# A windowed attention and MLP mixer kernel on one Trainium2 core: batch 3's first channel product by seven products of quarters, and new orders for the work and the loads

## The chip, the core and the metric

The kernel runs on one core of one Trainium2 chip. Its time is the device time of one execution in microseconds (us). The kernel before took 197.43 us, the median of three runs (196.32 to 197.87). The core has a matrix engine, TensorE (PE, with its weight loads shown apart as PEld), and VectorE (DVE), ScalarE (ACT) and GpSimd (POOL), which work on elements; SyncE (SP) only issues DMAs here. Matrix products land in PSUM, which is divided into banks; all other tiles lie in SBUF. Each engine takes its own queue of instructions in order and waits where an instruction's inputs, or the tile that it writes, are not free.

## What is computed

Attention with a sliding window of 128 and 4 sink positions (B=4, H=8, S=768, D=64), whose result x (4 x 768 x 512) goes through an MLP mixer:

```python
scores = (1/sqrt(D)) * q @ k.T
keep = (pos < n_sink) | ((rel >= 0) & (rel < window))       # rel = query - key
a = softmax(where(keep, scores, -1e9));  x = a @ v          # heads side by side: 4 x 768 x 512
xt = x.transpose(0, 2, 1)
h = relu(xt @ w_tok1) @ w_tok2                              # w_tok1 768x256, w_tok2 256x768
u = x + h.transpose(0, 2, 1)
out = u + relu(u @ w_ch1) @ w_ch2                           # w_ch1 512x1536, w_ch2 1536x512
```

The inputs and the output are float32 in DRAM; the products are taken in bf16 with float32 sums. The four batches are computed independently of each other.

## The kernel before

**Attention.** The work is done by pairs of heads: p = 0 to 15, four pairs to a batch. GpSimd's queue loads q, k and v of a pair with a cast to bf16 (`load_cast` L136, `load_v` L144) and the weights (`load_w` L169); pairs 0 to 3 come in by SP in float32 and are cast on an engine (L160). SP's queue also transposes q and k of pairs 8 to 15 by DMA (`turned_by_dma` L429, the DMA at L438); TensorE transposes the others. For a pair there are three bursts of scores (`scores`; a burst of 4 x 128 keys and queries of two heads goes into one "sc" tile of two banks), an exponential on ACT (L596), a mask multiplication on DVE (L604), the scores of the sink keys, the products with v (`pv` L664, `values`), and the division by the row sums on DVE. `sink_rows` copies the sink rows of v of a pair to where the products read them (L158 on ACT, L160 on DVE); it needs that pair's v to have landed.

**Mixer.** `mix_h` and `mix_u` make the token mixing, DVE adds x (L813), and u is turned into uT, by TensorE or, for batches 2 and 3, by a DMA of SP's queue (`transfer_u` L867). The first channel product makes v1T = relu(w_ch1' uT), 12 row tiles of 128 times 768 columns, in 24 units of four matmuls of 128 x 384 (`v1`, about L990), each evicted with the rectification by ACT or DVE (`relu`, L164, L166). The second channel product is direct in batch 0 (`out_part`, added to u at L1014, stored at L1020). In batches 1, 2 and 3 (`QUARTERED`) it is made by quarters: the operands are cut in two by two blocks, and seven products of sums of blocks replace eight products of blocks. The sums of v1 (L1206, DVE) and of w_ch2 (`sums_of_w` L1224, once) are made ahead. The products 1 to 7, each for three row tiles a, b, c, go to partial sums in PSUM that several products write into one after the other: 1, 6, 7 and 4 accumulate in one half of a bank, 5 and 3 in the other half of the same bank, 2 in a bank of its own. Between them the state of such an open sum is read out by DVE and added to the output tiles (L1078); the outputs are stored from SP's queue (L1107). `PRODUCTS` (L69) is their order.

**What sets the order.** The whole program is written out by a planner (class `Plan`). Each piece of work is an `Op` with an estimated cost on each engine that may do it and a list of what it needs. The order on TensorE is fixed by hand in two lists: `FIRST_BATCH`, and `MERGED` (L48), in which c0, c1, ... are the units of `mix_channels` and t0, t1, ... those of `attention_and_tokens`. So c0 to c47 are batch 0's channel products, c48 to c92 batch 1's, c93 to c137 batch 2's, c138 to c182 batch 3's. `LOADS` (L64) fixes the order on GpSimd's load queue; in it v9 is the values of pair 9, T and A are w_tok1 and w_tok2, C0 to C3 and D0 to D3 the quarters of w_ch1 and w_ch2. Everything else is put on an engine when it is ready by the estimates, and then stays in that place of the engine's queue. PSUM holds two "sc" tiles of two banks and four "mx" banks; the planner gives a unit the bank that comes free first.

In MERGED the units that the prediction names are: t27, the second burst of pair 8; t28, the first of pair 9; t32, the first of pair 10, which also takes the products of the sink rows of pair 9; t64, the first burst of pair 15, in the changed order the last with scores; c104, a v1 unit of batch 2 that in the changed order comes soon after t64; h0, batch 0's first token mixing, the first use of w_tok1.

The end of the kernel is batch 3's second product. Its last four products are 7c, 4c and 3c after 6c; of the last row tile's outputs each 128 x 256 quarter is added and stored apart, four stores of 128 KB.

Of the kernel before, what the change touches and what calls it, by code (L numbers as in the profile page):

```python
# [16 lines left out]
def kernel(  # L17
# [47 lines left out]
        "v1 v2 T0 v3 A0 k4 q4 q5 C0 v4 k5 C2 v5 q6 C1 k6 C3 k7 q7 D0 q8 v6 k8 D2 D1 D3 v7 k9 q9 q10 v8 k10 "  # L65
        "k11 q11 v9 v10 k12 k13 q12 q13 v11 v12 k14 q14 v13 k15 q15 v14 v15"
# [5 lines left out]
    SUMMED = 3  # L72
    NQ = 6
# [30 lines left out]
    def rows_of(pidx, n):  # L104
# [10 lines left out]
        "p (g f s) -> p g f s", g=4, f=HF,  # L115
    )
# [98 lines left out]
    kTb = [singles.tile([P, S], BF16, name=f"kT{n}") for n in range(NKB)]  # L215
    qTb = [singles.tile([P, S], BF16, name=f"qT{n}") for n in range(NKB)]
    pTb = [singles.tile([P, 2, NT, 2, P], BF16, name=f"pT{n}") for n in range(NPT)]
# [65 lines left out]
    class Plan:  # L283
# [142 lines left out]

    QH = NT // 2
# [434 lines left out]
    def transfer_u(b, g):  # L862

        for s0, n in [(0, 4), (4, 2)] if g else [(0, NT)]:
# [9 lines left out]
            for half in range(s0 // QH, (s0 + n - 1) // QH + 1):  # L874
                done.setdefault(("uT", b, half), []).append(op)
            plan.pending.append(op)
# [102 lines left out]
    def mix_channels(b):  # L979
# [60 lines left out]

        def quartered(b):
# [4 lines left out]
            units, made = [], {}  # L1046
# [10 lines left out]
            def w_summed(n):  # L1057
# [7 lines left out]
            v1_deps = {  # L1065
                "1": (0, 0), "2": (0, 1), "4": (1, 1),
            }
            sum_of = {"3": 3, "5": 0, "6": 1, "7": 2}
            w_sum_of = {"4": 3, "5": 0, "6": 1, "7": 2}
            w_of = {"1": 0, "2": 1, "3": 1}  # L1070
            steps = {}

            def add(name, i, st, g, src, first):
                def run(e):
                    n = (b * NT + st) % NO
                    o_sb = o_buf[n][:, ts(g, QC)]
                    ps = tiles["ps_q", b, i][:, src] if src < 2 else tiles["ps_z", b, i]
                    in_order(nc.vector.tensor_tensor(  # L1078
                        out=o_sb, in0=ps, in1=u_rows(b, st)[:, g] if first else o_sb, op=ALU.add,
                    ))  # L1080

                op = Op({"DVE": 425.0}, run)
# [4 lines left out]
                steps[name, i] = op  # L1087
                return op

            for i in range(QH):  # L1090
                lo, hi = i, i + QH
                add("r1", i, lo, 0, 0, True)
                add("c1", i, lo, 0, 2, False)
                add("r2", i, lo, 1, 0, True)
                add("c2", i, lo, 1, 1, False)
                add("r4", i, hi, 1, 0, True)
                add("c4", i, hi, 1, 1, False)
                add("c3", i, hi, 0, 0, True)
                for later, sooner in (("c1", "r1"), ("c2", "r2"), ("c4", "r4")):
                    steps[later, i].deps.append(steps[sooner, i])  # L1100
                for st, parts in ((lo, ("c1", "c2")), (hi, ("c3", "c4"))):
                    last_one = b == B - 1 and i == QH - 1

                    def store(e, st=st, g=None):
                        o_sb = o_buf[(b * NT + st) % NO]
                        cols = slice(0, DM) if g is None else ts(g, QC)
                        in_order(nc.sync.dma_start(out=out[b, ds(st * P, P), cols], in_=o_sb[:, cols]))  # L1107

                    if last_one:
                        for part in parts:  # L1110
                            g = 0 if part in ("c1", "c3") else 1
                            op = Op({"SP": 100.0}, lambda e, st=st, g=g: store(e, st, g), [steps[part, i]])
# [16 lines left out]
            def product(n, i):  # L1129
                def run():  # L1130
                    if n == "1":
                        tiles["ps_q", b, i] = bank("mx", 2, QC)
# [209 lines left out]
```

## Time and profile before

| | us |
|---|---|
| runs of the kernel before, median (lowest, highest) | 197.43 (196.32, 197.87) |
| the profiled execution | 197.73 |
| its span, first to last instruction | 195.8 |
| busy: PE / PEld | 185.8 / 129.0 |
| busy: DVE / ACT / POOL | 135.8 / 105.5 / 67.6 |
| moved by DMA | 26.32 MB, mean 134 GB/s |
| chain that ended last | PE 71%, DMA 17%, POOL 6%, DVE 2% |

The profile is of one execution. Its slices cut the span in 40 equal parts of 4.9 us, and a digit is the busy share of an engine in tenths (9 is 90% or more). The table of stretches gives, for a window of time, the busy time of PE, PEld, DVE, ACT and POOL with their counts, the granted TensorE clock, the share of DMA and GB/s. A row of the groups names engine and source line, operation, output tile <- input tile, shape, and count; behind the bar stand the summed time in us and the mean of one in ns, then the idle time ahead of them and what ended it. A row of the timeline starts with the time in us and a duration, and has in brackets the wait ahead of the instruction and what released it. "Issue" rows give a DMA's size and the median time from issue to landing.

### The profile page before, as it was taken

The numbers are of one execution on the slowest core, as the hardware profiler recorded it, in microseconds if no ns is written. First come the engines' busy times: TensorE is split into PE (matmuls) and PEld (weight loads), VectorE is DVE, ScalarE is ACT, GpSimd is POOL, SyncE is SP. The second block draws the span as 40 slices with busy tenths as digits, with TensorE's granted clock in tenths as the row PEclk, the third lists the DMA queues.
The fourth block names the chain that finished last, engine by engine and source line by source line (L and its number), as shares of the span: only waits on it lengthen the run. The fifth ranks groups of instructions, "written<-read, shape, count | busy, mean of one in ns | idle before, by whom it ended". The sixth has DMA issues, their size and how long they took to land.

```text
span 195.8 us, 5621 instructions
## 1 busy us (share of the span) xinstructions
PE 185.8 (95%) x2389; PEld 129.0 (66%) x2389; DVE 135.8 (69%) x295; ACT 105.5 (54%) x186; POOL 67.6 (35%) x86
## 2 busy tenths in 40 slices
PE   6798999999999999699999999999999999999992
PEld 2344995566655664466587888666678886667881
DVE  4597876879898646667987876865688772048571
ACT  4798768988825224669845407768551105773000
POOL 6099897779636943349440000000000000000000
PEclk9999999999999999999999999999999999999999
DMA  6999999999999999999999966500004425000035
GB/s 192 271 278 152 168 176 175 186 178 167 174 157 153 155 207 180 196 202 140 164 123 157 124 174 91 218 0 5 0 3 80 80 110 214 0 0 3 0 135 188
DMA packets 92361, 26.32 MB, mean 134 GB/s; under 512 B 82352, under 2 KB 89520, under 8 KB 92336
## 3 DMA queue, kind: packets, MB, share of 16 engines
q0 software_dynamic: 67232, 11.80, 77.4%
q1 hardware_dynamic: 25104, 14.17, 34.1%
q8 instruction: 18, 0.29, 0.6%
q14 instruction: 7, 0.06, 0.1%
HBM read 26.75 MB, written 6.29 MB: 169 GB/s over the span
## 4 chain that ended last, share of the span: by engine, by line
PE 71%; DMA 17%; POOL 6%; DVE 2%; issue 1%; ACT 1%; SPq 0%; DVEq 0%; POOLq 0%; ACTq 0%
PE ps_mx L151 66%; DMA v_aug<-in_v_dram 14%; PE ps_sc L151 4%; DMA v_sink_f<-in_v_dram 3%; POOL k_bf L136 2%; POOL v_aug L144 2%; POOL q_bf L136 1%; POOL w_tok L169 1%; PE ps_sc L511 1%; PE ps_mx L154 1%; ACT pT L596 1%; DVE u_sb L813 0%; SPq L230 0%; POOL k_bf L160 0%; POOL q_bf L160 0%
## 5 line engine op out<-in xcount | busy, mean ns | idle before, releaser
L151 PE MATMUL ps_mx<-uT,w_ch 128*128 128x384 bf16 x384 | 68.3, 326 | 0.0
L164 ACT ACTIVATE v1T<-ps_mx 128x384 bf16<-128x384 f32 x77 | 37.9, 492 | 34.8 <-PE ps_mx L151 34.5
L596 ACT ACTIVATE pT<-ps_sc 128x1024 bf16<-128x1024 f32 (+1 forms) x48 | 44.2, 953 | 16.7 <-PE ps_sc L151 8.9
L151 PEld LDWEIGHTS <-w_ch 128*128 128x128 bf16 x384 | 35.7, 98 | 22.5 <-issue 0.9
L151 PE MATMUL ps_mx<-w_ch,v1T 128*128 128x256 bf16 (+1 forms) x180 | 32.1, 315 | 0.0
L151 PEld LDWEIGHTS <-v1T 128*128 128x128 bf16 x234 | 22.0, 98 | 8.6 <-issue 0.5
L136 POOL DMA_DIRECT2D q_bf<-in_q_dram x24 | 19.8, 831 | 13.8 <-DMA v_aug<-in_v_dram 5.6
L151 PEld LDWEIGHTS <-early 128*128 128x128 bf16 x216 | 20.8, 98 | 2.8
L151 PEld LDWEIGHTS <-w_tok 128*128 128x128 bf16 x240 | 19.6, 98 | 3.7 <-DVE u_sb L813 0.3
L136 POOL DMA_DIRECT2D k_bf<-in_k_dram x24 | 19.9, 846 | 3.8 <-DMA v_aug<-in_v_dram 2.0
L151 PE MATMUL ps_mx<-w_sums,early 128*128 128x256 bf16 x162 | 20.3, 273 | 0.0
L1078 DVE TENSOR_TENSOR o_sb<-ps_mx,u_sb 128x256 f32<-128x256 f32 x36 | 14.9, 421 | 6.6 <-PE ps_mx L151 6.5
L144 POOL DMA_DIRECT2D v_aug<-in_v_dram x16 | 16.6, 1040 | 8.4 <-DMA w_ch<-in_moe_w_ch_dram 3.1
L813 DVE TENSOR_TENSOR u_sb<-ps_mx,x_sb 128x512 bf16<-128x512 f32 (+1 forms) x24 | 15.4, 654 | 5.2 <-PE ps_mx L151 5.1
L151 PEld LDWEIGHTS <-pT 128*128 128x128 bf16 x352 | 14.7, 98 | 3.2 <-issue 0.8
L1206 DVE TENSOR_TENSOR early<-v1T 128x1152 bf16<-128x1152 bf16 x12 | 8.8, 754 | 11.1 <-ACT v1T L164 11.1
L151 PE MATMUL ps_mx<-v_aug,pT 128*128 128x65 bf16 x352 | 16.1, 194 | 0.1
L604 DVE TENSOR_TENSOR pT<-pT,mask_main 128x768 bf16<-128x768 bf16 (+1 forms) x25 | 14.7, 615 | 2.0 <-ACT pT L596 2.0
L151 PE MATMUL ps_sc<-qT,kT 64*32 64x160 bf16 (+3 forms) x480 | 14.0, 232 | 1.9 <-ACT pT L596 1.8
L166 DVE TENSOR_SCALAR v1T<-ps_mx 128x384 bf16<-128x384 f32 x19 | 10.5, 554 | 7.2 <-PE ps_mx L151 6.8
L151 PE MATMUL ps_mx<-h1T,w_tok 128*128 128x256 bf16 (+1 forms) x120 | 14.4, 251 | 0.0
L151 PEld LDWEIGHTS <-kT 64*32 64x32 bf16 (+1 forms) x512 | 7.2, 91 | 10.4 <-issue 9.3
(74 smaller groups left out, 191.3 us busy)
## 6 DMA issues: line engine op xcount, KB each, us to landing
out_dram<-o_sb SPq DMA_DIRECT2D x22, 256.0 KB, 3.1
v_aug<-in_v_dram POOLq DMA_DIRECT2D x16, 192.0 KB, 7.9
w_ch<-in_moe_w_ch_dram POOLq DMA_DIRECT2D x8, 384.0 KB, 8.1
k_bf<-in_k_dram POOLq DMA_DIRECT2D x24, 96.0 KB, 7.9
q_bf<-in_q_dram POOLq DMA_DIRECT2D x24, 96.0 KB, 9.1
early<-in_q_dram SPq DMA_DIRECT2D x4, 384.0 KB, 5.9
early<-in_k_dram SPq DMA_DIRECT2D x4, 384.0 KB, 6.3
w_tok<-in_moe_w_tok_dram POOLq DMA_DIRECT2D x2, 384.0 KB, 7.3
```

Of the source, the lines that this page charges most:

```text
L136: in_order(nc.gpsimd.dma_start(out=out[:, h], in_=rows[:, h]))
L144: in_order(nc.gpsimd.dma_start(out=v_aug.rearrange("p i t d -> p (i t) d")[:, :, 0:D], in_=v[b].rearrange("h s d -> (h s) d")[2 * hp * S:2 ...
L151: in_order(nc.tensor.matmul(*args, skip_group_check=True, **kwargs))
L154: in_order(nc.tensor.transpose(out, in_, ident))
L164: in_order(nc.scalar.activation(out, in_, AF.Relu))
L166: in_order(nc.vector.tensor_scalar_max(out=out, in0=in_, scalar1=0.0))
L169: return in_order(nc.gpsimd.dma_start(out=out, in_=in_))
L596: in_order(nc.scalar.activation(part(tiles["pT", p][:, :, ds(2 * g, 2)]), of_keys(tiles["ps_s", p, g])[:, :, 0:width(g)], AF.Exp, scale=scale,
L604: in_order(nc.vector.tensor_tensor(out=pt, in0=pt, in1=m, op=ALU.mult))
L813: in_order(nc.vector.tensor_tensor(out=u_part(b, g, s0, n), in0=tiles["ps_u", b, g, s0], in1=x_sb[b][:, s0:s0 + n, c0:c0 + cn], op=ALU.add,))
L1078: in_order(nc.vector.tensor_tensor(out=o_sb, in0=ps, in1=u_rows(b, st)[:, g] if first else o_sb, op=ALU.add,))
L1206: lambda e, n=n, x=x, y=y, how=how: in_order(nc.vector.tensor_tensor(out=v1_sums[:, n, ds(j, SUMMED)], in0=of(x), in1=of(y), op=how,)), deps,
```

## The change

1. *Batch 3's first channel product by quarters* (`QUARTERED_V1`, new function `quartered_v1`). w_ch1' and uT are cut in two by two blocks; for each of 6 row tiles seven products of two matmuls (128 x 384 columns) stand for eight: 84 matmuls instead of 96. As in the second product, several products accumulate in one place, and the open sums are read between them. The first, second and fourth results are made of two places of PSUM: a copy to a float32 buffer ("snap", L158 or L160), an add of the second place on DVE, and a rectification into v1T ("over", on POOL, DVE or ACT as the planner finds). The third is rectified straight from PSUM ("last"). So 24 evictions go, and 18 snaps, 18 adds, 18 "overs" and 6 "lasts" come. The planner puts 17 snaps on ACT and one on DVE, 16 overs on POOL and two on ACT.
2. *New sums:* four of w_ch1 (128 x 1536, `sums_of_c1`, cost given for POOL alone) and four of uT (128 x 768, DVE). Their buffers and those of the open sums lie in tiles that attention has left: kT and qT, now one tile kqT, hold the sums of w_ch1, which therefore wait for the last scores of pairs 12 to 15; the three pT buffers hold the open sums; the second half of `early` holds the sums of u.
3. *Separate banks in batch 3.* The three open sums X, Y and Z lie in different banks (X and Y in the two banks of an "sc" tile for two row tiles of three, in "mx" banks for the third); the first product into Y starts its own sum, and the product that follows no longer waits for readers of the other sum.
4. *The end.* The last product (3c) is made in two groups of 128 columns, now 3c and 8c, six matmuls each; the row tile's second half is added and stored in two pieces, so that five stores stand at the end, the last of 64 KB.
5. *Orders:* MERGED is new from end to end (batch 3's units are now c138 to c201). In LOADS k4 comes ahead of v2 and T0, k5 ahead of q4 and C0, v5 ahead of v4, C3 ahead of v4, v10 ahead of v9, and others by a place or two. `sink_rows` of pair 9, on ACT before, is on DVE in the order that results, behind burst t28.
6. *The planner* no longer adds the estimated end of a PE unit where another PE unit needs it (same engine, same queue).

```diff
     LOADS = (
-        "v1 v2 T0 v3 A0 k4 q4 q5 C0 v4 k5 C2 v5 q6 C1 k6 C3 k7 q7 D0 q8 v6 k8 D2 D1 D3 v7 k9 q9 q10 v8 k10 "
-        "k11 q11 v9 v10 k12 k13 q12 q13 v11 v12 k14 q14 v13 k15 q15 v14 v15"
+        "v1 k4 v2 T0 v3 A0 k5 q4 C0 q5 C2 k6 C3 v5 v4 k7 q6 C1 q7 v6 D0 D2 k8 q8 D1 k9 D3 v7 q9 k10 q10 k11 q11 v8 v10 "
+        "v9 k12 q12 v11 q13 k13 q15 q14 v12 k14 k15 v13 v14 v15"
     )
...
+    QUARTERED_V1 = (3,)
...
+    u_sums = early.rearrange("p n h c -> p (n h c)")[:, HF * S:].bitcast(BF16).rearrange(
+        "p (g t k s) -> p g t k s", g=4, t=QH, k=2,
+    )
...
+    c1_sums = kqT.rearrange("p x n s -> p (x n s)").rearrange("p (g k f) -> p g k f", g=4, k=2)
+    open_v1 = pTs.rearrange("p n i k b q -> p (n i k b q)").bitcast(FP32).rearrange("p (n s) -> p n s", s=HS)
...
-                    t = max(t, x.done)
+                    if "PE" not in op.cost or "PE" not in x.cost:
+                        t = max(t, x.done)
...
+        PLACE = {"1": "X", "6": "X", "7": "X", "4": "X", "5": "Y", "3": "Y", "8": "Y", "2": "Z"}
...
+            def columns(n, i):
+                if b == B - 1 and i == QH - 1 and n in ("3", "8"):
+                    return slice(0, QC // 2) if n == "3" else slice(QC // 2, QC)
+                return slice(0, QC)
...
-            after = {"5": ("r1",), "6": ("r1",), "7": ("r2",), "4": ("r4", "c4"), "3": ("r4", "c4")}
+            after = {"5": ("r1",), "6": ("r1",), "7": ("r2",), "4": ("r4", "c4"), "3": ("r4", "c4"), "8": ("c4",)}
+            if apart:
+                after.update({"5": (), "4": ("r4",), "3": ("c4",)})
...
+        def quartered_v1(b):
...
+            for i in range(HF):
+                for n, (source, f, s) in enumerate((("Z", 0, 0), ("Y", 0, 1), ("Y", 1, 1))):
...
+                    def snap(e, i=i, n=n):
+                        copy(e, buffer(i, n), tiles["ps_w", b, i, "X"])
+
+                    def add(e, i=i, n=n, source=source):
+                        in_order(nc.vector.tensor_tensor(
+                            out=buffer(i, n), in0=tiles["ps_w", b, i, source], in1=buffer(i, n), op=ALU.add,
+                        ))
+
+                    def over(e, i=i, n=n, f=f, s=s):
+                        if e == "POOL":
+                            in_order(nc.gpsimd.tensor_scalar_max(out=v1_part(f, i, s), in0=buffer(i, n), scalar1=0.0))
+                        else:
+                            relu(e, v1_part(f, i, s), buffer(i, n))
...
+                    v = steps["v" + name, i] = Op({"POOL": 480.0, "DVE": 300.0, "ACT": 490.0}, over, [c, done["out", b - 1]])
...
+            after = {"6": ("r1",), "7": ("r2",), "4": ("r4",), "3": ("c4",)}
...
+            sums_of_u(b)
+            for j in range(0, HF, 3):
+                for n in "1256743":
+                    units += [product(n, i) for i in range(j, j + 3)]
+            for j in range(0, HF, SUMMED):
+                sums_of_v1(b, j)
+            return units
...
+            def run(e, n=n, x=x, y=y, how=how):
+                on = nc.gpsimd if e == "POOL" else nc.vector
+                in_order(on.tensor_tensor(out=c1_sums[:, n], in0=of(x), in1=of(y), op=how))
+
+            done["c1_sum", n] = Op({"POOL": 3400.0}, run, deps)
```

More of the change, by code (lines that the diff above doesn't have):

```diff
@@ L72 @@
     SUMMED = 3
+    QUARTERED_V1 = (3,)
+    QH = NT // 2
     NQ = 6
@@ L1087, in add, with store, run @@
                 steps[name, i] = op
+            def store(st, cols, parts):
+                def run(e):
+                    in_order(nc.sync.dma_start(
+                        out=out[b, ds(st * P, P), cols], in_=o_buf[(b * NT + st) % NO][:, cols],
+                    ))
+                op = Op({"SP": 430.0}, run, parts)
+                op.bulk, op.stores = 1.37 * (cols.stop - cols.start), True
                 return op
@@ L1091, in quartered @@
                 lo, hi = i, i + QH
[L1092 to L1098, printed above, removed]
+                ends = b == B - 1 and i == QH - 1
+                add("r1", i, lo, 0, "X", True)
+                add("c1", i, lo, 0, "Z", False)
@@ L1100, in quartered @@
                     steps[later, i].deps.append(steps[sooner, i])
[L1101 to L1112, printed above, removed]
-                            op.bulk, op.stores = 350.0, True
-                            steps["s" + part, i] = op
-                        continue
-                    op = Op({"SP": 100.0}, store, [steps[p, i] for p in parts])
-                    op.bulk, op.stores = 700.0, True
-                    done["st", b, st] = op
-                    steps["s" + parts[0], i] = op
@@ L1136, in run @@
+                    ps = tiles["ps_q", b, i, where][:, columns(n, i)]
                     left, right = factors[n]
                     for ft in range(HF):
-                        mm(ps, left(ft, i), right(ft), start=(n in "12" and ft == 0), stop=(ft == HF - 1))
-                deps = [steps[a, i] for a in after.get(n, ())]
+                        mm(
+                            ps, left(ft, i), right(ft)[:, columns(n, i)],
+                            start=((n in "12" or n == "5" and apart) and ft == 0), stop=(ft == HF - 1),
+                        )
@@ L1141, in product, with held @@
+                def held(*places):
+                    return [steps[r, i] for where in places for r in readers[where] if (r, i) in steps]
+                deps = [steps[a, i] for a in after[n]] if n in after else []
+                if n == "5":
+                    deps.append(made["1", i])
+                if n == "8":
+                    deps.append(made["3", i])
                 if n in v1_deps:
```

203 lines of the change are left out of this document (168 added, 35 removed), and 21 rows, old and new, of the table MERGED.

## The prediction

> **What bounds the kernel now.** I read the page's head and slices first, then busy time by stretches, then the chain of waits at the one place where TensorE idles in the middle of the run.
>
> ```profile
> span 195.8 us, 5621 instructions
> PE 185.8 (95%) x2389; PEld 129.0 (66%) x2389; DVE 135.8 (69%) x295; ACT 105.5 (54%) x186; POOL 67.6 (35%) x86
> PE   6798999999999999699999999999999999999992
> PEclk9999999999999999999999999999999999999999
> DMA  6999999999999999999999966500004425000035
> ...
> 10.00:20.00 10.00, 8.92 (x163) 4.85 (x160) 8.75 (x19) 9.02 (x14) 10.00 (x13) 1.00 1.66 211
> 79.00:82.00 3.00, 1.19 (x17) 0.72 (x16) 1.15 (x3) 2.20 (x5) 0.82 (x1) 1.00 1.87 192
> 162.40:175.60 13.20, 13.20 (x84) 7.95 (x83) 2.05 (x4) 9.34 (x19) 0.00 (x0) 1.00 0.18 66
> 175.60:191.90 16.30, 16.30 (x142) 13.69 (x140) 11.60 (x25) 2.46 (x5) 0.00 (x0) 1.00 0.17 63
> ```
>
> TensorE (PE) binds: 9s from slice 4 to the end but for one 6, at a granted clock of 1.00 in every stretch. The last two stretches are batch 3's two channel products with PE busy all the time. So a matmul taken out there is worth its full time, as long as nothing new is late. DMA is full for the first half and quiet afterwards, and GpSimd (POOL) does nothing in the second half.
>
> The 6 is this stall:
>
> ```profile
> 65.53 14.20 DMA v_aug<-in_v_dram
> 79.75 0.54 ACT L158 ACTIVATE v_sink<-v_aug 4x65 bf16<-4x65 bf16 x2 [3.30 <-DMA v_aug<-in_v_dram]
> 80.32 1.73 ACT L596 ACTIVATE pT<-ps_sc 128x1024 bf16<-128x1024 f32 x2
> 81.39 0.39 PE L151 MATMUL ps_sc<-qT,kT 64*128 64x256 bf16 x4 [1.81 <-ACT pT L596]
> ```
>
> The values of pair 9 land at 79.73. ScalarE (ACT), which takes its queue in order, sat 3.30 us in front of the copy of their sink rows; two exponentials queue behind it, and PE waits 1.81 us for a score bank.
>
> **The change part by part.** The sum is made against the profiled execution, 197.73 us at a span of 195.8; the median of the runs is 197.43, so it stands 0.30 above the median.
>
> *Seven products for eight.* Batch 3's first channel product was 24 units of 4 matmuls with 384 columns, 96 in all. Now it is 6 row tiles x 7 products x 2 matmuls, 84.
>
> ```profile
> 162.42 13.81 PE L151 MATMUL ps_mx<-uT,w_ch 128*128 128x384 bf16 x84
> 163.27 0.49 ACT L164 ACTIVATE v1T<-ps_mx 128x384 bf16<-128x384 f32 x1 [8.02 <-PE ps_mx L151]
> 163.92 0.49 ACT L164 ACTIVATE v1T<-ps_mx 128x384 bf16<-128x384 f32 x1 [0.16 <-PE ps_mx L151]
> ```
>
> The evictions start 0.65 us apart, one for each 4 matmuls: 0.163 us a matmul. 12 of them are 1.95 us. The last product in two column groups has 12 matmuls of 128 columns for 6 of 256; that is the same number of columns, and I add 0.02. Together -1.93.
>
> *What it costs beside PE.* Out go 24 evictions of v1. In come 18 copies of an open sum ("snap": 17 ACT, 1 VectorE), 18 adds on VectorE (DVE), 18 rectifications ("over": 16 POOL, 2 ACT), 6 last evictions on ACT, 4 sums of u on DVE, 4 sums of w_ch1 on POOL.
>
> ```profile
> L164 ACT ACTIVATE v1T<-ps_mx 128x384 bf16<-128x384 f32 x77 | 37.9, 492 | 34.8 <-PE ps_mx L151 34.5
> L813 DVE TENSOR_TENSOR u_sb<-ps_mx,x_sb 128x384 bf16<-128x384 f32 x6 | 3.2, 554 | 0.9 <-PE ps_mx L151 0.9
> L1206 DVE TENSOR_TENSOR early<-v1T 128x1152 bf16<-128x1152 bf16 x12 | 8.8, 754 | 11.1 <-ACT v1T L164 11.1
> L160 POOL CAST k_bf<-early 128x768 bf16<-128x768 f32 x1 | 0.9, 867 | 0.0
> L202 POOL TENSOR_SCALAR_AFFINE_SELECT mask_add<-mask_add 128x512 bf16<-128x512 bf16 x1 | 0.6, 637 | 0.7 <-DVE v_aug L212 0.7
> ```
>
> The tight half is row tiles 3 to 5: 21 products of 2 x 0.163, 6.8 us of PE. ACT has 13 operations there, 13 x 0.49 = 6.4. DVE has 9 adds of 0.55 and three sums of v1 of 0.75, 7.2, but two of these adds fall behind the last product. POOL's 16 rectifications read 384 elements: by the cast half of 0.867, 0.43, by the select 637 x 384/512 = 0.48, so 7.7 us at most, in the some 9 us between the last product of batch 2 (whose reads of v1T they must await) and the first of batch 3's second product. It fits on all three, each with a few tenths to spare, and the chain snap, product, snap runs over three row tiles by turns: one link is 0.33 of PE, 0.2 until ACT starts and 0.49 of ACT, about 1.0 us, against 1.95 us until the next product of the same row tile. Bounds: 0, if the spare tenths do, and 1.0, if the rectification that product 1a of the last stage waits for (the 13th on POOL) comes behind one slow operation on each engine. I take 0.2, nearer the end that these rows give.
>
> *The sums of w_ch1 on POOL.* Not shown before. The cast gives 1.13 ns an element for one input: 1536 elements are 1.7 us, and twice that, 3.5, if the two inputs are read in turn; four are 7 to 14 us. They can start when the scores of pair 15 are done, and the first product that needs one is over 25 us of PE work later. For the time itself: 0. Whether they hold up DVE:
>
> ```profile
> 8.97 0.56 DVE L160 CAST k_bf<-early 128x768 bf16<-128x768 f32 x1 [0.49 <-DMA early<-in_k_dram]
> 10.51 2.02 POOL L144 DMA_DIRECT2D v_aug<-in_v_dram  x2
> 10.85 1.04 DVE L160 CAST q_bf<-early 128x768 bf16<-128x768 f32 x1
> 11.81 1.11 DVE L160 CAST k_bf<-early 128x768 bf16<-128x768 f32 x1
> L604 DVE TENSOR_TENSOR pT<-pT,mask_first x14: 644/678/693, 18.2 to 131.7; 128x1024 bf16<-128x1024 bf16 x14
> ```
>
> A DVE cast takes 0.56 alone, and 1.04 and 1.11 when it begins inside POOL's 2.02 us of issuing: held until POOL is done. The two-input masks never exceed 0.69, though POOL issues beside many of them. Beside the new sums stand one mask and the sums of v1, two-input operations in SBUF like the masks. Bounds: 0 by the masks, and the price under rival 1, 1.6, if they are held as the casts are. The mask is the nearest in form; I take 0. The Trainium skill speaks against this: "SBUF — State Buffer", section "SBUF: two separate sides", says that a VectorE operation with two SBUF inputs and a GpSimd operation that reads SBUF exclude each other for a whole instruction, which the casts bear out for another pair and the masks, beside POOL work that reads little, neither show nor deny; by it the sum is 196.1 and not 194.5.
>
> *All orders anew, loads.* LOADS puts k4 ahead of v2 and w_tok1, and v10 ahead of v9.
>
> ```profile
> 12.52 0.84 POOL L169 DMA_DIRECT2D w_tok<-in_moe_w_tok_dram  x1
> w_tok<-in_moe_w_tok_dram POOLq DMA_DIRECT2D x1, 384.0 KB, 7.0
> 20.09 0.83 PE L151 MATMUL ps_mx<-x_sb,w_tok 128*128 128x128 bf16 x12
> GB/s 150 147 132 124 143 133 156 164 167 168 181 163 168 161 150 142 143 144 153 182 202 180 184 182 200 177 157 165 158 155 155 214 144 145 142 149 153 155 159 166
> v_aug<-in_v_dram POOLq DMA_DIRECT2D x2, 192.0 KB, 14.9
> POOL q_bf L136 <- DMA v_aug<-in_v_dram: 5.6, 3, 3.1
> ```
>
> w_tok1 lands at 12.52 + 7.0 = 19.5 and is first used at 20.09. k4 is 2 x 96 KB, at some 150 GB/s 1.3 us: it now lands at 20.8, and h0 waits 0.7. PE has no slack later to win that back; bounds 0 (if a later wait absorbs it) and 1.3. I take +0.7.
>
> v10 is 192 KB as well: v9 comes 1.1 to 3.1 us later (its bytes at 175 GB/s; the longest that POOL waited for a v), 80.8 to 82.8. Its sink rows are now copied by DVE after t28; behind them on DVE stand the normalisation of pair 8 and the masks of pair 9, and burst t32 waits for all of it. From t27, which PE reaches at about 74, to t32 are t27 itself, 4 out parts, 4 + 3 units of v1, two bursts and two value units, about 10 us: t32 is due at 84. So the stall goes: -1.8 (bounds -1.8 and 0), and next late is nothing by 1 us or more. Bursts of pairs 10, 11 and 15 come 4 to 13 us sooner than before; their transposes were issued 16 us or more ahead of use, so they keep slack.
>
> *The tail.*
>
> ```profile
> 190.48 0.82 PE L151 MATMUL ps_mx<-w_ch,early 128*128 128x256 bf16 x6
> 191.14 0.82 PE L151 MATMUL ps_mx<-w_sums,v1T 128*128 128x256 bf16 x6
> 192.00 0.42 DVE L1078 TENSOR_TENSOR o_sb<-ps_mx,o_sb 128x256 f32<-128x256 f32 x1 [0.89 <-PE ps_mx L151]
> 192.34 0.41 DVE L1078 TENSOR_TENSOR o_sb<-ps_mx,u_sb 128x256 f32<-128x256 f32 x1
> out_dram<-o_sb SPq DMA_DIRECT2D x4, 256.0 KB, 2.1
> out_dram<-o_sb SPq DMA_DIRECT2D x4, 128.0 KB, 1.8
> ```
>
> The add for product 3 sat 0.89 us until product 4, in the same bank, had ended too; then both adds ran, to 192.75. With separate banks only 128 columns are left to add behind the last matmul: 0.42 less 128 x 1.04 ns (0.42 for 256 columns, 0.55 for 384) is 0.29. The add ends 0.46 sooner; SP has a fifth store to issue just ahead, which I charge 0.16. The 64 KB store lands perhaps 0.15 sooner by the step from 2.1 to 1.8. Together -0.45 (bounds -0.6 and 0).
>
> Sum: 197.73 - 1.93 + 0.2 + 0 + 0.7 - 1.8 - 0.45 = 194.45: **194.5 us**.
>
> **The rivals.**
>
> 1. *DVE is held by POOL's sums of w_ch1.* In the new order sum 2 of v1 stands on DVE ahead of the add of u (batch 3, tiles 2 and 3), whose bank PE needs for c104. From t64 to c104 PE has six v1 units of 0.65, mix_h of 1.31, two value units, mix_u and pv, 6.9 us. POOL's second sum ends 0.2 + 2 x 3.5 = 7.2 after t64; then 0.75 and 0.69 on DVE make 8.6, so c104 is 1.6 to 1.7 late: 196.1. For: the casts. Against: the masks. At 1.7 us a sum it costs nothing.
>
> 2. *Loads move the stall.* If v9 lands past 84, DVE blocks at its sink rows and PE at t32. For: 14.9 us in flight at the worst. Against: the same bytes precede it but for v10. Another 2.5 us late gives 197.0.
>
> 3. *Slower: POOL's rectifications.* Product 1a of the last stage needs the 13th, on a queue that can't start before batch 2's last product; PE is there 9 us later. With d each, the delay is 13 x d - 9: nothing below 0.69, the time of before at 0.94 (3.2 us), over 1% slower from 1.1 us up, 199.7 or more. For: in-order queue, and sums of v1 beside them that may hold POOL 0.75 at a time. Against: 0.43 to 0.48 by the rows.
>
> 4. *The product gains nothing.* If a link of the snap chain takes over 1.95 us, twice what the rows give, its stage stays as long as before: 196.4.
>
> **How the numbers follow.** Forecast 0.50 (own range 193.0 to 195.4), rival 1 0.18, rival 2 0.14, rival 3 0.10, rival 4 0.08. 1% (what a measurement of this kernel can tell from no change) is 195.46 to 199.40. Faster: the forecast's 0.50 and 0.05 of rivals 1 and 4 at their low ends, 0.55. Slower: rival 3 and 0.02 of rival 2, 0.12. The rest, 0.33, is within 1%. The range 192.8 to 197.6 leaves out rival 3, 0.04 of rival 2 and 0.04 of forecasts whose gains come larger, 0.18.
>
> **What would show it.** Right: 84 matmuls of 384 columns at 0.163 in batch 3, no PE idle of a microsecond after 30 us, a first w_tok matmul at 20.8, POOL rectifications below 0.5, v1 sums at 0.75 beside POOL, a last add of 0.29. Wrong: DVE sums of 2 us or more beside POOL's (rival 1), a PE wait at t32 for sink rows (2), PE waiting for POOL ahead of product 1 (3), or gaps between the small products (4).

## The result

The changed kernel takes **205.77 us** (median of 4 runs: 205.17 to 205.80, and one of 212.4), the kernel before 197.4: a ratio of 1.042 (95% interval 1.037 to 1.048), 8.4 us slower. The ratios here and below leave out runs over 1.5% above the fastest of their kernel; the medians keep them. On a second chip, in the run a_again below, it is 1.057 (1.049 to 1.064). The forecast was 194.5 us and faster.

First the page of the changed kernel, head and slices, to set beside those of before.

```profile
span 204.0 us, 5658 instructions
PE 186.9 (92%) x2375; PEld 129.1 (63%) x2383; DVE 150.3 (74%) x314; ACT 107.7 (53%) x192; POOL 100.0 (49%) x106
PE   6799999999999999899999999698999999299892
POOL 6399796787726931397300019391000009989000
PEclk9999999999999999999999999999999999759999
```

The new low digits of PE stand in slices where POOL, which before did nothing in the second half, now has 9s, or just behind them: the 6 and the 8 between 127 and 143 us, and the 2 at 173 us. At the 2 the granted clock falls, which it does nowhere in the profile before (7, 5).

The busy time by stretches of the changed kernel (PE, PEld, DVE, ACT, POOL, then the clock) says the same in numbers; the stretches are: the last bursts of pairs 13 to 15 and the end of batch 2's first product; batch 2's second product; batch 3's first product from its middle; batch 3's second.

```profile
121.20:142.70 21.50, 18.99 (x252) 13.15 (x252) 19.77 (x28) 13.36 (x24) 13.10 (x4) 1.00 0.12 44
142.70:164.80 22.10, 22.10 (x183) 17.65 (x181) 16.80 (x35) 6.65 (x14) 0.00 (x0) 1.00 0.26 61
164.80:184.40 19.60, 15.67 (x85) 8.97 (x83) 11.92 (x22) 8.58 (x20) 14.80 (x13) 0.83 0.14 54
184.40:200.20 15.80, 14.50 (x134) 12.20 (x131) 11.96 (x29) 0.16 (x1) 4.30 (x4) 1.00 0.15 53
```

PE loses 2.5 us in the first, nothing in the second, 3.9 us and the clock in the third, 1.3 us in the last. Where POOL is idle, PE is full.

**First place: POOL's sums of w_ch1.** Timeline, POOL's rows, then DVE's, then PE's:

```profile
121.70 6.59 POOL L1397 TENSOR_TENSOR kqT<-w_ch 128x1536 bf16<-128x1536 bf16 x2 [22.93 <-PE ps_sc L157]
131.62 3.09 POOL L1397 TENSOR_TENSOR kqT<-kqT,w_ch 128x1536 bf16<-128x1536 bf16 x1 [3.33 <-issue]
134.79 3.42 POOL L1397 TENSOR_TENSOR kqT<-w_ch,kqT 128x1536 bf16<-128x1536 bf16 x1
...
123.55 1.79 DVE L613 TENSOR_TENSOR pTs<-pTs,mask_first 128x1024 bf16<-128x1024 bf16 x1
125.26 3.58 DVE L613 TENSOR_TENSOR pTs<-pTs,mask_main 128x1024 bf16<-128x1024 bf16 x1
128.76 0.55 DVE L172 TENSOR_SCALAR v1T<-ps_mx 128x384 bf16<-128x384 f32 x1
130.39 0.68 DVE L613 TENSOR_TENSOR pTs<-pTs,mask_first 128x1024 bf16<-128x1024 bf16 x1
132.79 2.47 DVE L613 TENSOR_TENSOR pTs<-pTs,mask_first 128x1024 bf16<-128x1024 bf16 x1
136.38 2.44 DVE L1371 TENSOR_TENSOR early<-v1T 128x1152 bf16<-128x1152 bf16 x1
138.75 0.68 DVE L822 TENSOR_TENSOR u_sb<-ps_mx,x_sb 128x512 bf16<-128x512 f32 x1
...
129.36 1.46 PE L157 MATMUL ps_mx<-uT,w_ch 128*128 128x384 bf16 x8 [1.60 <-DVE v1T L172]
139.48 2.11 PE L157 MATMUL ps_mx<-uT,w_ch 128*128 128x384 bf16 x12 [0.91 <-DVE u_sb L822]
```

A mask takes 0.68 us when POOL idles (130.39) and 1.79, 3.58 and 2.47 when it begins beside a sum: the last two end 0.55 us after that sum does (128.29 and 134.71). An eviction of v1 queues behind the mask of 3.58 us, and PE waits 1.60 us for it. In the same way a sum of v1 takes 2.44 us, where it takes 0.75 before, and ends 0.6 us after POOL's fourth sum; the add of u stands behind it, and PE waits 0.91 us for that add ahead of c104.

**Second place: POOL's rectifications.** Groups, then timeline:

```profile
L1259 POOL TENSOR_SCALAR v1T<-pTs 128x384 bf16<-128x384 f32 x16 | 19.1, 1217 | 31.4 <-PE ps_mx L157 30.3
...
168.49 9.10 POOL L1259 TENSOR_SCALAR v1T<-pTs 128x384 bf16<-128x384 f32 x8 [30.28 <-PE ps_mx L157]
174.22 1.05 DVE L1371 TENSOR_TENSOR early<-v1T 128x1152 bf16<-128x1152 bf16 x1 [2.69 <-POOL v1T L1259]
176.48 0.49 ACT L164 ACTIVATE pTs<-ps_mx 128x384 f32<-128x384 f32 x1 [4.29 <-POOL v1T L1259]
177.02 0.80 PE L157 MATMUL ps_mx<-early,kqT 128*128 128x384 bf16 x2 [3.73 <-ACT pTs L164]
177.62 2.12 PE L157 MATMUL ps_sc<-early,kqT 128*128 128x384 bf16 x6
180.30 8.40 POOL L1259 TENSOR_SCALAR v1T<-pTs 128x384 bf16<-128x384 f32 x7 [0.61 <-DVE pTs L1253]
188.74 0.76 DVE L1371 TENSOR_TENSOR early<-v1T 128x1152 bf16<-128x1152 bf16 x1 [2.19 <-POOL v1T L1259]
189.55 1.70 PE L157 MATMUL ps_sc<-w_sums,early 128*128 128x256 bf16 x14 [1.18 <-DVE early L1371]
```

One costs 1.22 us in the mean, where 0.43 to 0.48 was forecast. From its first start to its last end the queue runs 168.49 to 188.70, almost without a pause. It holds others up at three points: a snap on ACT waits for a free buffer of the ring of 12; a sum of v1 stands waiting at the head of DVE's queue with adds behind it; and product 6 of the last row tile waits for that snap. After 3.73 us without work the next matmuls take 0.32 us each instead of 0.163 (six in 2.12).

**Bookkeeping.** The order on TensorE is the same in the changed kernel and in most experiments, so the same matmul can be found in each. The mark used below is the burst at 121.21 us in the first profile: by its place in MERGED it is t52, the first burst of pair 13 (t56 and t64 follow at 126.81 and 131.09). The second end is the end of PE.

```profile
121.21 0.28 PE L157 MATMUL ps_sc<-kqT 64*128 64x256 bf16 x2
...
199.64 0.49 PE L157 MATMUL ps_mx<-w_ch,early 128*128 128x128 bf16 x6
```

| profile | to the mark | mark to PE's end | PE's end to the span's end |
|---|---|---|---|
| changed kernel | 121.2 | 78.9 | 3.8 |
| a_again (the same, other chip) | 123.0 | 78.9 | 3.8 |
| e1 | 124.6 | 74.0 | 3.8 |
| e2 / e3 | 125.7 / 125.7 | 80.1 / 76.8 | 3.8 / 3.8 |
| e4 | 127.0 | 71.2 | 3.8 |
| e5 / e12 (product direct, the same kernel twice) | 123.6 / 126.4 | **69.2** / 69.2 | 5.3 / 4.7 |
| e6 (old loads) | 129.1 | 78.9 | 3.8 |
| e7 / e10 | 122.7 / 124.9 | 83.0 / 78.3 | 3.9 / 3.8 |
| e8 | 121.9 | 71.6 | 3.8 |

The middle column repeats to 0.02 us where the kernel is the same behind the mark (changed kernel, a_again and e6; e5 and e12), while the first scatters by 6 us, e6 left aside, although the code up to the mark is nearly the same. So what happens behind the mark can be priced from single profiles, and what happens ahead of it can't. The kernel before has its bursts in another order; with the 69.2 of the direct product its mark would stand at 191.96 - 69.18 = 122.8 (124.2 in b_again). The 8.2 us between the two spans (195.8, 204.0) are then -1.6 ahead of the mark, +9.7 behind it, 0 at the end.

### The profile page after: what moved, and what is told of

Read it like the earlier page. It is cut to its first block, busy times and chain, and to the rows that moved or that the text cites. A ratio compares the mean times of both kernels' runs of the same rounds, so it can differ in the third digit from the quotient of the medians.

```text
span 204.0 us, 5658 instructions
## 1 busy us (share of the span) xinstructions
PE 186.9 (92%) x2375; PEld 129.1 (63%) x2383; DVE 150.3 (74%) x314; ACT 107.7 (53%) x192; POOL 100.0 (49%) x106
## 4 chain that ended last, share of the span: by engine, by line
PE 55%; DMA 19%; POOL 11%; DVE 9%; issue 1%; ACT 1%; POOLq 1%; SPq 1%
PE ps_mx L157 46%; PE ps_sc L157 8%; DMA v_aug<-in_v_dram 7%; POOL v1T L1259 7%; DMA q_bf<-in_q_dram 6%; DMA early<-in_k_dram 3%; DMA w_tok<-in_moe_w_tok_dram 3%; DVE pTs L613 3%; POOL v_aug L150 2%; DVE early L1371 2%; DVE x_sb L715 1%; DVE o_sb L1094 1%; POOL k_bf L142 1%; POOLq L1544 1%; SPq L129 1%
## 5 line engine op out<-in xcount | busy, mean ns | idle before, releaser
L157 PE MATMUL ps_mx<-uT,w_ch 128*128 128x384 bf16 x304 | 57.2, 328 | 3.2 <-DVE v1T L172 1.6
L605 ACT ACTIVATE pTs<-ps_sc 128x1024 bf16<-128x1024 f32 (+1 forms) x48 | 44.4, 957 | 13.5 <-PE ps_sc L157 13.3
L170 ACT ACTIVATE v1T<-ps_mx 128x384 bf16<-128x384 f32 x63 | 30.8, 492 | 23.6 <-PE ps_mx L157 22.6
L1259 POOL TENSOR_SCALAR v1T<-pTs 128x384 bf16<-128x384 f32 x16 | 19.1, 1217 | 31.4 <-PE ps_mx L157 30.3
L157 PEld LDWEIGHTS <-kqT 64*32 64x32 bf16 (+2 forms) x560 | 12.4, 93 | 15.9 <-issue 13.3
L613 DVE TENSOR_TENSOR pTs<-pTs,mask_main 128x768 bf16<-128x768 bf16 (+1 forms) x25 | 17.8, 730 | 1.6 <-ACT pTs L605 1.6
L1397 POOL TENSOR_TENSOR kqT<-w_ch 128x1536 bf16<-128x1536 bf16 x2 | 6.6, 3318 | 22.9 <-PE ps_sc L157 22.9
L157 PE MATMUL ps_mx<-v_aug,pTs 128*128 128x65 bf16 x352 | 16.4, 194 | 0.0
L157 PEld LDWEIGHTS <-pTs 128*128 128x128 bf16 x352 | 14.3, 98 | 2.4 <-issue 0.4
L157 PE MATMUL ps_sc<-kqT 64*32 64x160 bf16 (+3 forms) x480 | 14.3, 232 | 0.5 <-DVE ps_sc L538 0.3
```

The source lines that it names most:

```text
L157: in_order(nc.tensor.matmul(*args, skip_group_check=True, **kwargs))
L170: in_order(nc.scalar.activation(out, in_, AF.Relu))
L605: in_order(nc.scalar.activation(part(tiles["pT", p][:, :, ds(2 * g, 2)]), of_keys(tiles["ps_s", p, g])[:, :, 0:width(g)], AF.Exp, scale=scale,
L613: in_order(nc.vector.tensor_tensor(out=pt, in0=pt, in1=m, op=ALU.mult))
L1259: in_order(nc.gpsimd.tensor_scalar_max(out=v1_part(f, i, s), in0=buffer(i, n), scalar1=0.0))
L1397: in_order(on.tensor_tensor(out=c1_sums[:, n], in0=of(x), in1=of(y), op=how))
```

## The experiments

**a_again and b_again**: no edit.

> The changed kernel once more, unchanged, beside the others on one chip. In the four experiments so far PE came to the burst at 121.5 us (time of the first profile) 3.4 to 5.8 us later than in that profile, though their instructions up to there are the same. If that is the scatter of the loads, this run too has all its difference from the first profile ahead of 121.5 us, with w_tok1 or the values of pairs 7 to 9 landing later, and from 121.5 us to the end it agrees within 0.2 us (78.7 us to the last product). If the first profile was the rule, it is the same within 0.3 us throughout.

> The kernel before, for a second profile of it. If the old orders of loads and of the work have the slack that the new ones lack, its PE is within 1 us of the first profile of before at 120 us, though loads land at times that differ by as much as between the runs of the changed kernel. If it scatters as much, 3 us or more apart, the loads don't tell the kernels apart.

a_again: 209.0 us beside 197.5 of the kernel before on that chip. Ahead of the mark it is 1.8 us later than the first profile, and behind it the same within 0.02, as the first theory had it. b_again, a single run: 199.02 us. PE is up to 0.5 us ahead of the first profile until 78 us, and from 85 us on 1.45 us behind it. The loads are not the reason: the old stall at pair 9's values is 1.87 us here and was 1.81 there. But behind it the granted clock was halved for 3.4 us (a row stands below at e10), which it was not in the first profile. So neither of the two theories fits: the old orders scatter too, here by the clock.

**e1**: the rectifications off POOL.

```diff
-v = ... Op({"POOL": 480.0, "DVE": 300.0, "ACT": 490.0}, over, [c, done["out", b - 1]])
+v = ... Op({"DVE": 300.0, "ACT": 490.0}, over, [c, done["out", b - 1]])
```

> The changed kernel, but the 16 rectifications of open sums that GpSimd did are done by ACT (0.49 us each) and VectorE; the order on TensorE is the same. Theory A (GpSimd's rectifications, 1.16 us each, bound the end: PE lost 8.9 us after 168 us to them): most of that comes back, less up to 2 us that the extra work on ACT and VectorE costs in the tight half, so 197 to 199 us. Theory B (the chain of copies, adds and products over separate banks is itself too slow, and GpSimd is only the last to be seen): ACT and VectorE have more to do than before, so 204 us or more.

204.68 us, ratio 1.040 (1.033 to 1.046): by the total theory B. But the profile's mark is 3.4 us later than the first one's; behind the mark 4.96 us are gone. Theory A holds for the cause, and the 2 us that ACT and DVE were allowed are 2.8 (beside e4).

**e2 and e3**: the sums of w_ch1 on DVE; e3 with e1's edit as well.

```diff
+            deps += [done["u", B - 1, 1, 4]]
-            done["c1_sum", n] = Op({"POOL": 3400.0}, run, deps)
+            done["c1_sum", n] = Op({"DVE": 1000.0}, run, deps)
```

> The changed kernel, but the four sums of w_ch1 are made by VectorE (about 1.0 us each, by 0.75 us for 1152 columns) after batch 3's u is complete, not by GpSimd beside the last masks; rectifications stay on GpSimd. Theory A (GpSimd's two-input sums hold VectorE's masks for up to 2.9 us, which cost PE 1.76 us at 127.6 and 1.08 us at 138.2): both waits go, masks at 0.68 us or less throughout, 203 us (205.8 less 2.8). Theory B (the masks are late for another reason, such as the new order of the bursts): the waits stay, 205 to 206.5 us.

> Both of the edits above together: GpSimd does nothing after its last load. If the two causes are separate and are all that was wrong, the sum of their gains, 194.5 to 196 us, below the kernel before (197.4). If something else of the change costs time as well, more than 197.4 us.

211.0 us (1.069, 1.064 to 1.075) for e2; e3's four runs spread from 203.8 to 211.1 (median 207.9), too far for a ratio. Both totals are misses, by my edit: the sum of u that I made the four sums wait for is not the last in PE's order, and the later ones stood behind the four.

```profile
150.88 0.95 DVE L1398 TENSOR_TENSOR kqT<-w_ch 128x1536 bf16<-128x1536 bf16 x1
155.23 0.95 DVE L1398 TENSOR_TENSOR kqT<-w_ch,kqT 128x1536 bf16<-128x1536 bf16 x1
...
156.83 0.82 PE L157 MATMUL ps_mx<-uT,w_ch 128*128 128x384 bf16 x4 [3.87 <-DVE u_sb L822]
```

What they were made for they show all the same: the two waits of PE beside POOL's sums are gone in both (the 252 matmuls behind the mark take 18.83 us instead of 21.67, and 18.83 in e5 too, which has no such sums), the masks are back at 0.68. POOL's sums cost 2.84 us. One of them takes DVE 0.95 us, POOL 3.1 to 3.5.

**e4**: what is slow about the rectification on POOL. It leaves the rectification of 16 tiles out.

```diff
-in_order(nc.gpsimd.tensor_scalar_max(out=v1_part(f, i, s), in0=buffer(i, n), scalar1=0.0))
+copy(e, v1_part(f, i, s), buffer(i, n))
```

> The changed kernel, but GpSimd's 16 rectifications are plain copies from float32 to bf16 of the same tiles (the rectification of these 16 tiles is left out). If it is the operation that is slow on GpSimd, a copy takes 0.45 us (half of the 0.85 us of a 128x768 cast) and the end gains most of 8.9 us: 197 to 198.5 us. If it is that the DVE sums hold GpSimd, or that GpSimd is slow on these float32 tiles whatever it does, a copy takes 1.1 us as well and the time stays at 205.8 us.

```profile
174.26 1.85 POOL L166 CAST v1T<-pTs 128x384 bf16<-128x384 f32 x4 [30.25 <-PE ps_mx L157]
178.59 0.99 POOL L166 CAST v1T<-pTs 128x384 bf16<-128x384 f32 x1 [0.17 <-DVE pTs L1253]
```

It is the operation: a copy takes 0.46 us (four in 1.85) on the same tiles where the maximum takes 1.14 (eight in 9.10). A copy by itself takes 0.51, beside a sum of v1 on DVE 0.99: the two engines hold each other here too. Time 200.87 us (1.016, 1.008 to 1.024), with a mark 5.8 us late; behind the mark 7.7 us are gone, which is the price of the slow operation.

**e5**: the product undone, all else of the change kept (`QUARTERED_V1 = ()`, batch 3's units in their old order).

> The changed kernel with batch 3's first channel product direct again (24 units of four matmuls, batch 3's units in the old order); new orders up to there, new loads, separate banks and the split last product stay. Theory A (GpSimd's work for the quarters costs 8.9 and 2.8 us, the product saves 1.9): 205.8 - 11.7 + 1.9 = 196 us, and up to 3 us more where loads land late. Theory B (the new orders are what costs): 203 us or more.

200.38 us, ratio 1.009 (1.003 to 1.015), runs from 197.6 to 202.6: between the two theories. From the mark to PE's end 69.18 with PE busy throughout. So the product costs 78.93 - 69.18 = 9.75 us, and the rest of the change 0.9% by the ratio (2.9 us by the medians) where by the prediction 1.55 us were to be gained (0.7 - 1.8 - 0.45). In this profile and in e12's one store's issue took 1.8 and 1.3 us on SP, and the end is 1.5 and 0.9 us longer than elsewhere; why, no run here tells.

**e6**: the loads in the old order under the new order of work.

> The changed kernel with the loads in the order of before; the order on TensorE is the same but for the place of a few transposes ahead of 45 us. If the new loads cost 1 to 4 us in the first 120 us, as their waits at w_tok1 and at 63 to 84 us say, 202 to 204.5 us. If the new order of work needs the new loads, more waits before 100 us and 206 us or more. From 121.5 us on nothing changes by either.

213.6 us (1.079, 1.073 to 1.085): PE waits 5.0 us for a quarter of w_ch1 at 36 us. The second of the two outcomes: the new order of work needs the new loads. The old order of work with the new loads was not run.

**e7 and e10**: is the low clock a cost of its own? 24 matmuls with discarded results, in e7 in product 5 of the last row tile, in e10 in that of row tile 3.

```diff
+if n == "5" and i == 3:
+    for _ in range(24):
+        mm(tiles["ps_w", b, i, where]..., left(0, i), right(0), start=True, stop=True)
```

> The changed kernel plus 24 matmuls of 128x384 (3.9 us of PE) whose results are thrown away, put where PE otherwise stood idle 3.7 us ahead of product 6 of the last row tile (product 5 of that tile, which holds them, moved ahead of it). In the first profile the 18 matmuls after that idle stretch took 0.32 us each, twice the usual. If idleness lowers the clock, they now take 0.163 us, and the 2.9 us come off if PE sets the end there: about 3 us less between 164.8 us and the end (35.4 us before). If GpSimd's queue of 16 rectifications sets the end, which runs from 168.5 to 188.7 us with only 1.1 us of waits in it, at most 1.2 us come off though PE runs at full clock. If the clock drops for another reason, the matmuls stay at 0.32 us and 3.9 us are added.

> The changed kernel plus 24 matmuls of 128x384 with discarded results (3.9 us of PE), written into the still unused bank half that product 5 of row tile 3 of the last six opens just ahead of PE's 3.7 us of idleness. PE then has work through the idle stretch. If idleness lowers the clock, all matmuls after it take 0.163 us; if that loss is on the path, PE's time from the mark at 164.8 us to its end is 32.5 us or so (35.4 in the changed kernel); if GpSimd's 16 rectifications set that time whatever PE's clock is, 34.2 to 35.4 us; if the clock falls without idleness, 35.4 us or more with matmuls at 0.32 us.

e7 missed its aim: its bank was itself waiting for DVE, so PE idled 2.5 us and then had the 3.9 us to do (212.5 us, 1.080, 1.072 to 1.087). There too the clock was low after it: 28 matmuls behind the wait took 6.14 us, some 1.4 more than at 0.163 each. In e10, a single run of 209.11 us, PE has work and keeps its clock. Stretches of the changed kernel, then of e10:

```profile
173.00:177.00 4.00, 0.29 (x2) 0.07 (x1) 2.04 (x3) 0.52 (x2) 4.00 (x5) 0.89 0.00 0
177.00:183.00 6.00, 5.98 (x20) 2.75 (x20) 3.90 (x7) 3.22 (x8) 4.88 (x5) 0.51 0.00 0
```

```profile
176.00:180.00 4.00, 4.00 (x27) 2.41 (x25) 1.52 (x2) 0.00 (x0) 4.00 (x4) 1.00 0.00 0
180.00:184.00 4.00, 3.81 (x24) 2.17 (x23) 3.69 (x7) 3.39 (x8) 3.49 (x4) 1.00 0.02 4
```

With 3.9 us of useless matmuls it comes from mark to end 0.65 us sooner (78.28). So idleness halves the clock, which "TensorE: Matmul & The Clock Gate", Part 1, of the Trainium skill states with a window of some 3.4 us, but the 2.9 us that the slow matmuls cost PE lay almost all beside POOL's queue.

How long PE has to idle for it does not come out as one number. Stretches behind a wait of 1.87 us (b_again), of 1.77 us (e12) and of 3.87 us (e2):

```profile
81.80:85.20 3.40, 3.40 (x30) 2.26 (x29) 2.32 (x7) 1.36 (x3) 0.82 (x1) 0.50 1.59 240
121.90:125.30 3.40, 3.40 (x18) 2.44 (x17) 1.78 (x4) 0.23 (x1) 0.00 (x0) 0.50 0.55 209
156.80:160.20 3.40, 3.37 (x29) 2.84 (x30) 1.69 (x4) 0.49 (x1) 0.00 (x0) 1.00 0.42 77
```

The two shorter waits were followed by 3.4 us at half clock, which is the length of that window; the longest was not, nor were the 1.81 us of the kernel before and the 1.60 us at 129.4 us of the changed one. In the changed kernel the low clock lasts twice as long, 6.8 us. What decides, no run here tells.

**e8**: nothing on POOL but loads. Sums of w_ch1 on DVE behind all sums of u; open sums written as bf16; rectified by DVE and ACT.

```diff
+def summed_v1(i, n):
+    return buffer(i, n).bitcast(BF16)[:, 0:HS]
-    out=buffer(i, n), in0=tiles["ps_w", b, i, source], in1=buffer(i, n), op=ALU.add,
+    out=summed_v1(i, n), in0=tiles["ps_w", b, i, source], in1=buffer(i, n), op=ALU.add,
```

> The changed kernel with nothing left on GpSimd but its loads: the sums of w_ch1 on VectorE after the last sum of u of batch 3, the open sums written as bf16, their rectification on VectorE (an estimated 0.2 us from bf16) and ACT. If GpSimd's two works were all that was wrong from 121 us on, PE's time from the burst at 121.2 us to its end is 68 to 70.5 us (78.9 in the changed kernel, 69.2 with the product direct, 67.3 by PE's work alone); the whole is then 198 to 201 us, since what the loads cost ahead of 121 us stays. If ACT and VectorE can't carry the chain, 71 us or more from 121.2 us.

200.07 us (1.014, 1.007 to 1.020), as the whole was expected, but 71.58 from mark to end: just past the bound that was set for "ACT and DVE can't carry the chain". PE's worst waits are now there:

```profile
PE ps_mx L157 <- ACT pTs L164: 1.3, 1, 1.3
PE ps_sc L157 <- ACT v1T L170: 1.1, 2, 0.9
PE ps_sc L157 <- DVE pTs L1256: 0.7, 1, 0.7
...
L1256 DVE TENSOR_TENSOR pTs<-ps_mx,pTs 128x384 bf16<-128x384 f32 x10 | 5.4, 551 | 0.2 <-PE ps_mx L157 0.2
L170 ACT ACTIVATE v1T<-pTs 128x384 bf16<-128x384 bf16 x14 | 6.6, 518 | 2.2 <-PE ps_mx L157 2.1
```

The waits are for snaps, rectifications and adds. The direct product needs 24 evictions of about 0.5 us, 12 us. The quarters need 18 snaps (0.49), 18 adds (0.55), 18 rectifications (0.25 to 0.52), 6 last evictions and eight sums (0.55 and 0.95): 8.8 + 9.9 + 8 + 2.9 + 6 = 36 us on two engines, to save 1.95 us of a third.

**e9**: e8's product under the old orders of work and loads.

> The kernel before in its own orders of work and loads up to the end of batch 2, and batch 3's first product by quarters as in the run before (nothing on GpSimd), separate banks and split last product. If the old orders carry it and the product yields PE's 1.93 us less the about 1.1 us that its chain has cost so far, 196.0 to 197.0 us where the kernel before takes 197.4; if the chain eats the whole, 197.5 us or more.

202.3 us (1.026, 1.022 to 1.031), the second of the two outcomes and well past its bound. Here the product isn't woven into the end of batch 2, and PE waits 0.7 to 1.0 us in six places between 159 and 183 us, for snaps, adds, a rectification and a sum of w_ch1.

**e11 and e12**: e11 is the kernel before with only the separate banks, the split last product and the planner's edit; e12 is e5 again.

> The kernel before with its own orders and loads, and only the separate banks of batch 3's second product and the split last product. The prediction had 0.45 us of gain for it; the changed kernel's profile shows 3.86 us from PE's end to the end of the span where before has 3.84, since five stores follow each other at 0.4 to 0.6 us on SP. So 197.2 to 197.6 us if that holds, 197.0 if the prediction does, and 199 us or more if this part is what makes the changed kernel with the product undone slow.

> The changed kernel with batch 3's first product direct, a second time (200.4 us in the first, over ten runs from 197.6 to 202.6), beside the run before on the same chip. If the new orders lose to the loads, 2 to 4 us more than the run before, all of it ahead of the burst at 121.2 us, in waits for w_tok1, for the values of pairs 7 to 9 and for transposed k of the last pairs, and with more scatter than the kernel before. If the first result was that chip's, the two agree within 1 us.

e11: 196.09 us over 12 runs (194.7 to 197.1), ratio 0.996 (0.993 to 1.000): the fastest kernel here, if barely, and well below the 197.0 to 197.6 that were expected. e12: 200.2 us (196.6 to 203.0), ratio 1.006 (1.002 to 1.010), the medians 4.1 us apart and the ratios 1.0%, with intervals that do not touch. So the new orders are slower. That they scatter more is not shown: e12's runs spread over 6.4 us and e11's over 2.3, but those of the kernel before, on the same chip and with the old orders, over 5.0 (195.6 to 200.6). The waits of PE that differ, from e12, e4 and e11:

```profile
121.04 0.39 PE L157 MATMUL ps_mx<-kqT 64*32 64x512 bf16 x2 [1.77 <-DMA kqT<-k_bf]
```

```profile
PE ps_sc L157 <- ACT pTs L605: 1.4, 1, 1.4
PE ps_mx L157 <- DMA w_tok<-in_moe_w_tok_dram: 1.1, 2, 1.0
PE ps_mx L157 <- ACT uT L164: 1.0, 1, 1.0
PE ps_mx L157 <- DMA v_aug<-in_v_dram: 1.0, 2, 0.5
```

```profile
PE ps_mx L504 <- POOL k_bf L166: 0.4, 1, 0.4
PE ps_mx L160 <- DVE u_sb L822: 0.3, 1, 0.3
```

Under the new orders PE waits for w_tok1, values and transposed k; in e11 nothing of that is left above 0.4 us. e12 and e5 are the same kernel, and PE is within 0.04 us in both from 76 to 119 us; the 2.8 us between their marks are 1.1 us that e12 waits longer for that transposed k (1.77 and 0.68), and the rest 3.4 us at half clock behind that wait.

## Why the prediction was wrong

Its terms against what they measured, in us; the measured column adds up, but for rounding, to the 8.2 between the spans:

| term | predicted | measured | by |
|---|---|---|---|
| 12 matmuls fewer, split product | -1.93 | -1.9 | 84 matmuls, 0.163 each at full clock |
| quarter chain beside PE | +0.2 | +1.1 | e4 less POOL's sums: 68.4, against 69.18 - 1.93 |
| POOL's rectifications | 0 (rival 3) | +7.7 | changed kernel less e4 |
| POOL's sums of w_ch1 | 0 (rival 1: 1.6) | +2.8 | e2, e3, e5 |
| loads and orders ahead of the mark | -1.1 | -1.6 in this profile, up to +4.2 in others | mark against 122.8 |
| the end | -0.45 | 0 | 3.8 us in both |

- **The step that failed most is the price of a rectification on POOL**, "by the cast half of 0.867, 0.43, by the select 0.48". Both rows are of other operations. A copy did cost 0.46; the maximum costs 1.14. The bound was drawn from two rows of which neither was this operation, and the term's range was cut there, though the sentence on rival 3 knew that the time of before is reached at 0.94. By its formula, 13 d - 9 with the mean of 1.22 is 6.9 us; measured are 7.7 (7.1 in e10, where the clock stays up). What the formula left out is that the queue is felt before the last stage: it already stops PE for 3.73 us by the ring of buffers, and after that stop the clock is low.
- **Rival 1 came true as well**, and step by step in the place that it names: two sums of POOL end 7.1 us after t64 (7.2 forecast), the sum of v1 is held until then, the add of u stands behind it, and c104 waits 0.91 us (1.6 to 1.7 forecast). What it missed is the larger part. The sums were to start "when the scores of pair 15 are done", beside one mask. But the first two, which write where k and q of pairs 12 and 13 lay, start at 121.70, right behind the last scores of pair 13, and hold masks of pairs 13 and 15; from there come the 1.60 us. The choice of 0 went by masks that had run beside POOL's DMA issues only. The Trainium skill's rule ("SBUF — State Buffer", "SBUF: two separate sides"), which spoke against the choice, agrees with the rows above: masks and a sum of v1 beside POOL's sums, sums of v1 beside its rectifications (1.05 us for 0.75).
- **The two came together.** The prediction gave them 0.18 and 0.10 apart from each other; both hang on one thing, unknown prices of POOL work, and should have been one case.
- **The loads**: the stall at pair 9 shrank from 1.8 to 0.7 us in this profile, and w_tok1 cost 0.3; this was right to a few tenths. What was wrong is the claim that nothing else is late: the new orders leave no slack to loads that land at other times in each run: the copy of sink rows that waits for values at 60.4 us in this profile (5.4 us) is at 65.6 in e4. The transposed k "issued 16 us or more ahead" was late by 0.7 to 1.8 us in e1, e5, e7 and e12.
- **The end**: the last add did end 0.33 us after PE, as forecast for separate banks. In the changed kernel five stores at 0.4 to 0.6 us each queue on SP and take it back, against the 0.16 that was charged; in e11, where the earlier stores go out sooner, the end is 3.3 us, 0.55 less than before, about the 0.45 that was forecast.
- **The quarter chain** was counted as fitting "with a few tenths to spare". With rectifications that ACT and DVE must do, e8 shows 2.4 us of loss against the direct product where 1.9 of gain were due. So the outcome of rival 4, no gain, comes without POOL too; whether by its reason, a link of the snap chain of over 1.95 us, no run separates. With POOL's rectifications at the price of a copy (e4, less POOL's sums) 0.8 us of gain would be left.

Left open: why e11 gains 0.6 us more than its end explains. In its profile the stall at pair 9 is gone; DVE copies that pair's sink rows there (at 78.44 us), as in the changed kernel, but the values also landed 1.3 us sooner than in the profile before, so the two are not told apart. Open are also the long store issues of e5 and e12, and which waits are followed by the low clock.

## What to carry to other kernels

Price an operation on GpSimd by a row of the same operation, or by a run of it alone; a copy of the same tile was off by 2.5 times. Count a step of this kind (seven products of sums for eight, known as Strassen's) by the reads and writes of its open sums on every engine, not by the matmuls that it saves: in e8 24 us more on two engines for 1.95 us of PE. And compare reordered kernels from a common instruction onwards, because what lies behind the mark repeats to 0.02 us here, while what lies ahead of it, with the loads, scatters by several.

## What the hardware showed unexpectedly

GpSimd's maximum of 128 x 384 float32 elements with a constant takes 1.14 us; its copy 0.46; ACT's rectification of the same tile 0.52 and DVE's 0.35 (e1). A VectorE operation that reads two SBUF tiles and a GpSimd operation that reads SBUF exclude each other in both directions: 0.68 became up to 3.58 us on VectorE, 0.51 became 0.99 on GpSimd. After a wait TensorE can run at half clock for 3.4 us or twice that: after 1.77, 1.87, 2.5 and 3.73 us it did, after 1.60, 1.81 and in one case 3.87 it did not. The same program can so differ by 1.5 us from one execution to the next (before and b_again).
